# Three ring slots of 62 KiB rows in place of four of 39 KiB in a one-core decode block

## The chip, the cores and the metric

The kernel runs on one core of a Trainium2 chip, in one launch. A time is the device time of that core in microseconds (us); the time before is the median of three runs, 214.47 us (214.38 to 214.60). A profile is one execution recorded by the hardware profiler. The engines are PE (TensorE matmuls; PEld is its weight load), DVE (VectorE), ACT (ScalarE), POOL (GpSimd) and SP (SyncE), which here issues nearly all transfers. Sixteen DMA engines move the data.

## The reference

One decode step for 4 tokens: attention over the last 1024 positions of a cache with 8 key/value heads (two query heads each), then an MLP, all in float32.

```python
# x: (4, 1, 448); k_cache, v_cache: (4, 8, 4096, 256); wq: (448, 4096); wo: (4096, 448); w1: (448, 1792); w2: (1792, 448)
W = min(4096, max(256, Sk // 4))                       # 1024
q = (layernorm(x) @ wq).reshape(B, 1, 16, 256).transpose(0, 2, 1, 3)
k = repeat(k_cache[:, :, Sk - W:, :], 2, axis=1)
v = repeat(v_cache[:, :, Sk - W:, :], 2, axis=1)
p = softmax(einsum("bhqd,bhkd->bhqk", q, k) * 256 ** -0.5)
h = x + einsum("bhqk,bhkd->bhqd", p, v).transpose(0, 2, 1, 3).reshape(B, 1, 4096) @ wo
h2 = h + gelu_tanh(layernorm(h) @ w1 + b1) @ w2 + b2
```

## The kernel before

**What is loaded.** For each head g there are its keys (32 KiB per partition, `CACHE` = 8192 floats), its values (the same), a slice of wq and a slice of wo (7 KiB per partition each, `WEIGHTS` = 1792 floats). The host packs them as the kernel wants them: `kq[g - 1]` holds the keys of head g and behind them the query weights of head g + 1; `vo[g]` holds the values of head g and behind them its output weights. So a load is 128 rows of 39936 bytes, 4992 KB in all. Twelve such loads (k1, v0, k2, v1, ... k6, v5) make up the middle of the kernel.

**Where it goes.** The pool `ring` has two tags, "k" and "v", with two buffers each: four slots of 39936 bytes per partition. A load can be issued when the load that had its slot two before it has been used up. The program's order on SP is the order of the loads:

```python
    for g in range(HKV - 2):
        kt, wqt = load_k(g + 1)
        vt, wot = load_v(g)
        p, rec_next = scores(g + 1, kt)
        project_q(g + 2, wqt)
        transpose_p(g + 1, p)
        po = po_tile(g)
        values(g, vt, po)
        transposed_output(g, po, rec)
        add_output(g, wot)
        rec = rec_next
```

**What is done with it.** `scores` (line 182) multiplies the queries with the keys in two halves of 512 positions and takes the maxima (DVE); ACT makes the exponentials `p`. `project_q` (159, 165) makes the next head's queries. `transpose_p` (207) turns `p` into `pT`. `values` (219) multiplies `pT` with the values in four pairs of chunks into `po`. `transposed_output` (236, 240) scales and transposes `po` into `oT`; `add_output` (248) adds its product with the output weights to `acc`. PE runs its instructions in the order in which the program is written; the other engines' order is found by the scheduler.

**The start.** wq0 (with the transposed input), k0 (with most of the query weights of head 1) and a small rest wq1_last are loaded first.

**The end.** After the loop come k7 (4096 KB), v6 with its output weights (4992 KB), v7 in three pieces (1024, 2048, 1024 KB), its output weights wo7 (896 KB), w1 in two pieces (1792, 1344 KB) and w2 in three (1792, 896, 448 KB), all still through the four slots. PE then runs scores(7), two idle products (`keep_warm`, line 308, bf16 on zeros), the transposes of `p7`, ten idle products, values(6), the first quarter of values(7), the output of head 6, the rest of values(7), its output, the layer norm, the w1 product (388), the gelu, and the w2 product, of which chunks 0 to 7 are line 421 and chunks 8 to 13 line 431. Line 431 first needs the second piece of w2, then (from chunk 12) the third; the sum `py`, the residual `res` and the store end the kernel.

**Completion counters.** Transfers use eight completion counters in turn (DMAHW0 to DMAHW7 in the listings below); a transfer whose counter is still in use waits for the earlier transfer on it to land.

Of the kernel before, what the change touches and what calls it, by code (L numbers as in the profile page):

```python
# [8 lines left out]
F32 = mybir.dt.float32  # L9
# [3 lines left out]
AX = mybir.AxisListType  # L13
PSUM = bass.MemoryType.PSUM

B, D = 4, 448
# [3 lines left out]
F = 1792  # L20
P = 128
H = P // 2
ND = 4
# [2 lines left out]
FQ = F // 4  # L26
Q = 32
CACHE = NKC * B * DH
WEIGHTS = 4 * D
EPS = 1e-5  # L30
SCALE = DH ** -0.5

@with_exitstack
def block_kernel(ctx: ExitStack, tc, rows, wq0, k0, wq1, kq, vo, w1, w2, out):
    nc = tc.nc
    const = ctx.enter_context(tc.tile_pool(name="const", bufs=1))
    ring = ctx.enter_context(tc.tile_pool(name="ring", bufs=2))
    work = ctx.enter_context(tc.tile_pool(name="work", bufs=2))
    once = ctx.enter_context(tc.tile_pool(name="once", bufs=1))
    ps_s = ctx.enter_context(tc.tile_pool(name="ps_s", bufs=2, space=PSUM))  # L40
# [4 lines left out]

    def load(kind, src, pieces, name):
        t = ring.tile([P, CACHE + WEIGHTS], F32, tag=kind, name=name)
        at = 0  # L50
        for n in pieces:
            nc.sync.dma_start(t[:, at : at + n], src[:, at : at + n])  # L52
            at += n
        return t


    def wq_parts(t, last=None):
        parts = [(a, yT[:, a, :], slice(0, 512), t[:, a * 512 : (a + 1) * 512]) for a in range(3)]
        if last is not None:
            return parts + [(3, yT[:H, 3, :], slice(0, 512), last)]  # L60
        for i in range(2):
            parts.append((3, yT[:, 3 + i, :], slice(i * 2 * P, (i + 1) * 2 * P), t[:, 3 * 512 :]))
        return parts


    def load_k(g):
        half = CACHE // 2
        if g == 0:
            t = load("k", k0, (CACHE + 3 * 512,), "k0")


            for i in range(2):
                nc.sync.dma_start(
                    wq1_last[i * Q : (i + 1) * Q, :], wq1[i].rearrange("e (p c) -> e p c", c=512)[:, :4, :]
                )
            last = wq1_last
        else:
            pieces = (CACHE + WEIGHTS,) if g + 1 < HKV else (CACHE,)
            t = load("k", kq[g - 1], pieces, f"k{g}")
            last = None  # L80
        kt = [t[:, i * half : (i + 1) * half].rearrange("p (c b k) -> p c b k", c=2, b=B) for i in range(2)]
        return kt, wq_parts(t[:, CACHE:], last) if g + 1 < HKV else None


    def load_v(g):
        pieces = (CACHE + WEIGHTS,)
        if g == HKV - 1:
            pieces = (CACHE // 4, CACHE // 2, CACHE // 4, WEIGHTS)
        t = load("v", vo[g], pieces, f"v{g}")
        v = t[:, :CACHE].rearrange("p (c b d) -> p c b d", c=NKC, b=B)  # L90
        return [v[:, c : c + 2] for c in range(0, NKC, 2)], t[:, CACHE:].rearrange("p (j e) -> p j e", j=4)


    ident = const.tile([P, P], F32, name="ident")
# [61 lines left out]
    def project_q(g, parts):  # L156
        pq = ps_m.tile([P, 512], F32, tag="m", name=f"pq{g}")
        for j, y, cols, w in parts:
            nc.tensor.matmul(pq[j * Q : (j + 1) * Q, cols], y, w, start=True, stop=True)  # L159
# [12 lines left out]
        for i in range(2):  # L172
            nc.vector.tensor_copy(qT[g % 2][:, :, :, i * REP : (i + 1) * REP], src)

    def scores(g, kt):
        mx = work.tile([P, 2], F32, tag="mx", name=f"mx{g}")
        halves = []
        for h in range(2):
            s = ps_s.tile([P, 512], F32, tag="s", name=f"s{g}_{h}")
            for c in range(2):  # L180
                for b in range(B):
                    nc.tensor.matmul(  # L182
                        s[b * Q : (b + 1) * Q, :], qT[g % 2][:, c, b, :], kt[h][:, c, b, :],
                        start=(c == 0), stop=(c == 1),
                    )
            nc.vector.reduce_max(mx[:, h : h + 1], s, axis=AX.X)  # L186
            halves.append(s)
        nm = work.tile([P, 1], F32, tag="nm", name=f"nm{g}")
        nc.vector.tensor_max(nm, mx[:, 0:1], mx[:, 1:2])
        nc.vector.tensor_scalar_mul(nm, nm, -SCALE)  # L190
        p = work.tile([P, 2 * 512], F32, tag="p", name=f"p{g}")
        sums = work.tile([P, 2], F32, tag="sums", name=f"sums{g}")
        for h in range(2):
            nc.scalar.activation(  # L194
                p[:, h * 512 : (h + 1) * 512], halves[h], AF.Exp, bias=nm, scale=SCALE,
                accum_out=sums[:, h : h + 1],
            )
        rec = work.tile([P, 1], F32, tag="rec", name=f"rec{g}")
        nc.vector.tensor_add(rec, sums[:, 0:1], sums[:, 1:2])
        nc.vector.reciprocal(rec, rec)  # L200
        return p, rec

    def transpose_p(g, p):
        for h in range(2):
            pt = ps_t.tile([P, 4, P], F32, tag="t", name=f"ppt{g}_{h}")
            for c in range(4):
                nc.tensor.transpose(pt[:, c, :], p[:, (4 * h + c) * P : (4 * h + c + 1) * P], ident)  # L207

            src = pt.rearrange("p (c i) (b q) -> p c i b q", i=2, b=B)
            for i in range(2):  # L210
                nc.vector.tensor_copy(  # L211
                    pT[g % 2][:, 2 * h : 2 * h + 2, :, i * REP : (i + 1) * REP], src[:, :, i, :, :REP]
                )


    def values(g, vt, po, pairs=range(NKC // 2)):
        for c in pairs:
            for b in range(B):
                nc.tensor.matmul(  # L219
                    po[b * Q : (b + 1) * Q], pT[g % 2][:, c, b, :], vt[c][:, :, b, :],  # L220
                    start=(c == 0), stop=(c == NKC // 2 - 1),
                )
# [11 lines left out]
    def transposed_output(g, po, rec):  # L234
        o = work.tile([P, 2, DH], F32, tag="o", name=f"o{g}")
        nc.vector.tensor_scalar_mul(o, po, rec)  # L236
# [7 lines left out]
        nc.vector.tensor_add(dst, dst, src[:, 1, :, REP : 2 * REP])  # L244

    def add_output(g, wt):
        for i in range(4):
            nc.tensor.matmul(  # L248
                acc[i * Q : (i + 1) * Q, :], oT[g % 2][:, i, :], wt[:, i, :],
                start=(g == 0), stop=(g == HKV - 2),  # L250
            )
# [7 lines left out]
        return pool.tile([P, 2, DH], F32, tag=tag, name=f"po{g}")  # L259


    t = load("v", wq0, (WEIGHTS + ND * B,), "wq0")
    wqt = wq_parts(t[:, :WEIGHTS])
    xT = t[:, WEIGHTS : WEIGHTS + ND * B].rearrange("p (a b) -> p a b", a=ND)
# [8 lines left out]
    nc.vector.tensor_mul(yT[H:, 4, :B], d[H:, 3, :], rx[H:, :])  # L273
    project_q(0, wqt)

    kt, wqt = load_k(0)
    p, rec = scores(0, kt)
    project_q(1, wqt)
    transpose_p(0, p)
    for g in range(HKV - 2):  # L280
        kt, wqt = load_k(g + 1)
        vt, wot = load_v(g)
        p, rec_next = scores(g + 1, kt)
        project_q(g + 2, wqt)
        transpose_p(g + 1, p)
        po = po_tile(g)
        values(g, vt, po)
        transposed_output(g, po, rec)
        add_output(g, wot)
        rec = rec_next  # L290
# [12 lines left out]

# [201 lines left out]
```

## Time and profile before

| | before |
|---|---|
| median of three runs | 214.47 us |
| profiled execution, its span | 212.9 us |
| the median less the span | 1.57 us |
| scores, L182, PE busy | 42.3 us |
| values, L219, PE busy | 40.0 us |
| idle time of PE before L182 ended by a load of keys | 22.6 us |
| idle time of PE before L219 ended by a load of values | 19.6 us |
| bytes read from HBM | 88.26 MB |

The span is the time from the first to the last recorded instruction; a run's time also has what lies around it. In the timeline a row gives the start, the length, the engine, the line, the operation, the count, and in brackets the idle time of the engine just before it and what ended that. One float32 product of 128x512 shows as two matmul records, so that the 16 products of a whole `scores` or `values` are 32 records. "PEclk" in a row of stages is the clock that the throttle granted PE, 1.00 being the full one.

### The profile page before, as it was taken

How to read it: one execution, taken by the hardware profiler on the slowest of the kernel's cores; microseconds unless marked ns; L12 is line 12 of the kernel's file. 1: busy time of each engine (PE TensorE's matmuls, PEld its weight loads, DVE VectorE, ACT ScalarE, POOL GpSimd, SP SyncE). 2: the span in 40 equal slices, each digit the busy share in tenths (PEclk: the TensorE clock that was granted, in tenths of full speed). 3: DMA queues.
4: the chain of work that ended last, by engine and by line, in shares of the span. 5: the costliest groups of instructions: out<-in, count | busy, mean ns of one | idle time of the engine just before them, and what ended most of it. 6: DMA issues, size and time to landing. Idle time of an engine off the chain costs nothing.

```text
span 212.9 us, 2306 instructions
## 1 busy us (share of the span) xinstructions
PE 137.9 (65%) x971; PEld 49.1 (23%) x971; DVE 39.2 (18%) x167; ACT 21.0 (10%) x52; POOL 5.6 (3%) x17
## 2 busy tenths in 40 slices
PE   0456868093886739583986348382948476798994
PEld 0322233021231212211231113120222123234432
DVE  1420324001130202210130104110230231022320
ACT  0210213000030000300030003000030001000311
POOL 6100000000000000000000000000000000000110
PEclk9999999669597966969599859979797999699999
DMA  7999998999989999999999999999989999999991
GB/s 291 426 399 469 398 465 378 459 465 390 458 378 465 465 390 458 398 446 465 390 458 405 443 465 386 465 413 428 461 375 468 440 428 390 417 418 433 424 390 60
DMA packets 3865, 88.46 MB, mean 415 GB/s; under 512 B 448, under 2 KB 576, under 8 KB 1168
## 3 DMA queue, kind: packets, MB, share of 16 engines
q1 hardware_dynamic: 3824, 88.29, 96.9%
q8 instruction: 7, 0.11, 0.2%
q10 hardware_dynamic: 32, 0.05, 0.1%
q14 instruction: 2, 0.02, 0.0%
HBM read 88.26 MB, written 0.07 MB: 415 GB/s over the span
## 4 chain that ended last, share of the span: by engine, by line
DMA 85%; PE 11%; DVE 2%; issue 0%; SPq 0%
DMA v<-vo 65%; DMA w<-w 12%; DMA k<-k 8%; PE po L219 8%; PE acc L248 1%; DVE o L236 1%; PE pot L240 1%; PE py L431 1%; DVE oT L243 0%; DVE oT L244 0%; SPq L52 0%; DVE res L437 0%; PE py L256 0%
## 5 line engine op out<-in xcount | busy, mean ns | idle before, releaser
L182 PE MATMUL s<-k,qT 128*32 128x512 f32 x256 | 42.3, 822 | 24.7 <-DMA k<-kq 22.6
L219 PE MATMUL po<-v,pT 128*32 128x512 f32 x256 | 40.0, 772 | 19.6 <-DMA v<-vo 19.6
L186 DVE TENSOR_REDUCE mx<-s 128x1 f32<-128x512 f32 x16 | 11.1, 691 | 67.4 <-PE s L182 67.4
L182 PEld LDWEIGHTS s<-k,qT 128*32 128x32 f32 x256 | 10.0, 146 | 54.7 <-issue 29.4
L219 PEld LDWEIGHTS po<-v,pT 128*32 128x32 f32 x256 | 10.7, 135 | 42.3 <-issue 31.4
L161 ACT COPY qs<-pq 128x512 f32<-128x512 f32 x8 | 4.7, 586 | 135.8 <-PE pq L159 135.8
L236 DVE TENSOR_SCALAR o<-po,rec 128x512 f32<-128x512 f32 x8 | 6.0, 750 | 60.2 <-PE po L219 60.2
L194 ACT ACTIVATE p<-s,nm 128x512 f32<-128x512 f32 x16 | 10.9, 690 | 18.4 <-DVE nm L190 18.4
L207 PE MATMUL ppt<-ident,p 128*128 128x128 f32 x64 | 10.5, 286 | 2.0 <-ACT p L194 1.7
L165 PE MATMUL pqt<-ident,qs 128*128 128x128 f32 x32 | 5.7, 304 | 6.2 <-ACT qs L161 6.2
L240 PE MATMUL pot<-ident,o 128*128 128x128 f32 x32 | 5.2, 286 | 5.7 <-DVE o L236 5.7
L248 PE MATMUL acc<-v,oT 128*32 128x448 f32 x56 | 6.7, 551 | 3.3 <-DVE oT L244 3.3
L207 PEld LDWEIGHTS ppt<-ident,p 128*128 128x128 f32 x64 | 6.7, 140 | 6.0 <-ACT p L194 6.0
L159 PE MATMUL pq<-k,yT 128*32 128x512 f32 (+1 forms) x66 | 7.3, 515 | 0.0
L308 PE MATMUL warm<-idle 128*32 128x512 bf16 x25 | 7.3, 382 | 0.0
L240 PEld LDWEIGHTS pot<-ident,o 128*128 128x128 f32 x32 | 3.3, 140 | 13.0 <-DVE o L236 13.0
L165 PEld LDWEIGHTS pqt<-ident,qs 128*128 128x128 f32 x32 | 3.6, 150 | 10.9 <-ACT qs L161 9.1
L153 POOL TENSOR_TENSOR r<-ve_r,mhalf 128x1 f32<-128x1 f32 x2 | 1.1, 544 | 191.9 <-DVE ve_r L152 191.9
L211 DVE COPY pT<-ppt 128x16 f32<-128x16 f32 x32 | 4.7, 170 | 4.7 <-PE ppt L207 4.7
L159 PEld LDWEIGHTS pq<-k,yT 128*32 128x32 f32 x66 | 3.1, 110 | 6.1 <-issue 4.8
L138 PE MATMUL pm_x<-wq,mean 128*128 128x12 f32 x2 | 0.6, 363 | 5.8 <-DMA wq<-wq 5.8
L167 DVE TENSOR_REDUCE sm<-pqt 128x16 f32<-128x64 f32 x8 | 1.8, 225 | 13.0 <-PE pqt L165 13.0
(101 smaller groups left out, 60.9 us busy)
## 6 DMA issues: line engine op xcount, KB each, us to landing
v<-vo SPq DMA_DIRECT2D x7, 4992.0 KB, 31.8
k<-kq SPq DMA_DIRECT2D x6, 4992.0 KB, 32.0
k<-k SPq DMA_DIRECT2D x1, 4864.0 KB, 16.3
k<-kq SPq DMA_DIRECT2D x1, 4096.0 KB
w<-w SPq DMA_DIRECT2D x2, 1792.0 KB
v<-vo SPq DMA_DIRECT2D x2, 1024.0 KB, 22.2
v<-vo SPq DMA_DIRECT2D x1, 2048.0 KB
w<-w SPq DMA_DIRECT2D x1, 1344.0 KB
```

The lines of the kernel that those rows point to most:

```text
L159: nc.tensor.matmul(pq[j * Q : (j + 1) * Q, cols], y, w, start=True, stop=True)
L161: nc.scalar.copy(qs, pq)
L165: nc.tensor.transpose(pt[:, i, :], qs[:, i * P : (i + 1) * P], ident)
L182: nc.tensor.matmul(s[b * Q : (b + 1) * Q, :], qT[g % 2][:, c, b, :], kt[h][:, c, b, :], start=(c == 0), stop=(c == 1),)
L186: nc.vector.reduce_max(mx[:, h : h + 1], s, axis=AX.X)
L194: nc.scalar.activation(p[:, h * 512 : (h + 1) * 512], halves[h], AF.Exp, bias=nm, scale=SCALE, accum_out=sums[:, h : h + 1],)
L207: nc.tensor.transpose(pt[:, c, :], p[:, (4 * h + c) * P : (4 * h + c + 1) * P], ident)
L219: nc.tensor.matmul(po[b * Q : (b + 1) * Q], pT[g % 2][:, c, b, :], vt[c][:, :, b, :], start=(c == 0), stop=(c == NKC // 2 - 1),)
L236: nc.vector.tensor_scalar_mul(o, po, rec)
L240: nc.tensor.transpose(pt[:, i, c], o[:, i, c * P : (c + 1) * P], ident)
L248: nc.tensor.matmul(acc[i * Q : (i + 1) * Q, :], oT[g % 2][:, i, :], wt[:, i, :], start=(g == 0), stop=(g == HKV - 2),)
L308: nc.tensor.matmul(warm[:Q], idle[:, :Q], idle, start=True, stop=True)
```

## The change

The pool `ring` gets one tag with three buffers of 63488 bytes per partition. The keys, values and weights of three heads at a time are cut into four loads, in the order in which they are used:

| load | floats per partition | holds |
|---|---|---|
| la | 14080 (56320 bytes) | keys g+1, query weights g+2, first half of values g |
| lb | 14080 (56320 bytes) | second half of values g, output weights g, keys g+2 |
| lc | 15872 (63488 bytes) | query weights g+3, values g+1, output weights g+1, first half of keys g+3 |
| ld | 15872 (63488 bytes) | second half of keys g+3, query weights g+4, values g+2, output weights g+2 |

They run for g = 0 and g = 3: eight loads with the bytes of the twelve. The products are written in the order of the parts: `values` of a head may be split over two loads (la, lb), and `scores` likewise (lc, ld), for which `scores` is cut into `scores_half` and `softmax`. wq0 and k0 share the first slot. At the end k7 and w1 share one slot, v6 and the output weights of heads 6 and 7 a second, v7 and w2 the third. The order and the sizes of those last loads stay as they were; k7 becomes an array of its own. `p` has one buffer in place of two. The area kept for software-made DMA descriptors is set to 1024 bytes.

```diff
+HALF = CACHE // 2
 WEIGHTS = 4 * D
+SLOT = CACHE + 2 * WEIGHTS + HALF
...
-    ring = ctx.enter_context(tc.tile_pool(name="ring", bufs=2))
+    ring = ctx.enter_context(tc.tile_pool(name="ring", bufs=3))
...
-    def load(kind, src, pieces, name):
-        t = ring.tile([P, CACHE + WEIGHTS], F32, tag=kind, name=name)
+    def slot(name):
+        return ring.tile([P, SLOT], F32, tag="r", name=name)
+
+    def load(t, at, src, pieces=None):
+        dst = t[:, at : at + src.shape[-1]]
         at = 0
-        for n in pieces:
-            nc.sync.dma_start(t[:, at : at + n], src[:, at : at + n])
+        for n in pieces or (src.shape[-1],):
+            nc.sync.dma_start(dst[:, at : at + n], src[:, at : at + n])
             at += n
-        return t
+        return dst
+
+    def cut(t, sizes):
+        parts, at = [], 0
+        for n in sizes:
+            parts.append(t[:, at : at + n])
+            at += n
+        return parts
...
-        p = work.tile([P, 2 * 512], F32, tag="p", name=f"p{g}")
+        p = once.tile([P, 2 * 512], F32, tag="p", name=f"p{g}")
...
-    for g in range(HKV - 2):
-        kt, wqt = load_k(g + 1)
-        vt, wot = load_v(g)
-        p, rec_next = scores(g + 1, kt)
-        project_q(g + 2, wqt)
+    def finish(g, po, rec, wt):
+        transposed_output(g, po, rec)
+        add_output(g, output_weights(wt))
+
+    for g in (0, 3):
+        ka, kb, wqt, va = cut(load(slot(f"ta{g}"), 0, la[g // 3]), (HALF, HALF, WEIGHTS, HALF))
+        p, rec_next = scores(g + 1, [keys(ka), keys(kb)])
+        project_q(g + 2, wq_parts(wqt))
         transpose_p(g + 1, p)
         po = po_tile(g)
-        values(g, vt, po)
-        transposed_output(g, po, rec)
-        add_output(g, wot)
-        rec = rec_next
+        va = chunks(va)
+        values(g, va, po, range(0, 2))
+
+        vb, wot, ka, kb = cut(load(slot(f"tb{g}"), 0, lb[g // 3]), (HALF, WEIGHTS, HALF, HALF))
+        values(g, va + chunks(vb), po, range(2, 4))
+        p, rec_then = scores(g + 2, [keys(ka), keys(kb)])
+        finish(g, po, rec, wot)
+        transpose_p(g + 2, p)
+
+        wqt, v, wot, ka = cut(load(slot(f"tc{g}"), 0, lc[g // 3]), (WEIGHTS, CACHE, WEIGHTS, HALF))
+        project_q(g + 3, wq_parts(wqt))
+        po = po_tile(g + 1)
+        values(g + 1, chunks(v), po)
+        first_half = scores_half(g + 3, 0, keys(ka))
+        finish(g + 1, po, rec_next, wot)
+
+        kb, wqt, v, wot = cut(load(slot(f"td{g}"), 0, ld[g // 3]), (HALF, WEIGHTS, CACHE, WEIGHTS))
+        p, rec = softmax(g + 3, [first_half, scores_half(g + 3, 1, keys(kb))])
+        project_q(g + 4, wq_parts(wqt))
+        transpose_p(g + 3, p)
+        po = po_tile(g + 2)
+        values(g + 2, chunks(v), po)
+        finish(g + 2, po, rec_then, wot)
...
-    kt, _ = load_k(g + 1)
-    vt, wot = load_v(g)
-    vt_last, wo_last = load_v(g + 1)
-    t = load("k", w1, (2 * F, F + F // 2), "w1")
-    w1t = [t[:, a * F : min((a + 1) * F, 3 * F + F // 2)] for a in range(ND)]
-    t = load("k", w2, (8 * D, 4 * D, 2 * D), "w2")
-    w2t = [t[:, c * D : (c + 1) * D] for c in range(NFC)]
+    e = [slot(f"te{i}") for i in range(3)]
+    kt = [keys(t) for t in cut(load(e[0], 0, k7), (HALF, HALF))]
+    v, wot = cut(load(e[1], 0, vo[0]), (CACHE, WEIGHTS))
+    vt, wot = chunks(v), output_weights(wot)
+    vt_last = chunks(load(e[2], 0, vo[1][:, :CACHE], (CACHE // 4, CACHE // 2, CACHE // 4)))
+    wo_last = output_weights(load(e[1], CACHE + WEIGHTS, vo[1][:, CACHE:]))
+    w1t = cut(load(e[0], CACHE, w1, (2 * F, F + F // 2)), (F, F, F, F // 2))
+    w2t = cut(load(e[2], CACHE, w2, (8 * D, 4 * D, 2 * D)), NFC * (D,))
```

Two places of the order matter below. The first is SP's queue from the last loads of the loop to the last piece of v7. A row gives the line, the operation, the tile and its source, and what the issue waits for: DMAHW is a completion counter, PE that engine's progress. Before:

```order
L52 DMA k6_719<-kq 128x9984 [waits DMAHW6_49,PE_49]
L52 DMA v5_721<-vo 128x9984 [waits DMAHW7_49,PE_49]
L52 DMA k7_815<-kq 128x8192 [waits DMAHW0_49,PE_49]
L52 DMA v6_817<-vo 128x9984 [waits DMAHW1_49,PE_49]
L52 DMA v7_819<-vo 128x2048 [waits DMAHW3_49,PE_49]
```

And with the change:

```order
L57 DMA tc3_669<-lc 128x15872 [waits DMAHW6_49,DMAHW3_49,PE_49]
L57 DMA td3_729<-ld 128x15872 [waits DMAHW7_49,DMAHW4_49,PE_49]
L57 DMA te0_813<-k7 128x8192 [waits DMAHW5_49,PE_49]
L57 DMA te1_814<-vo 128x9984 [waits DMAHW6_49,PE_49]
L57 DMA te2_815<-vo 128x2048 [waits DMAHW7_49,PE_49]
```

The first piece of v7 (te2) takes over the slot of td3, the last load of the loop, and is issued when PE has done the last product that reads td3; before it took the slot of v5.

The second place is PE's queue from the last load of the loop to scores(7). Before, with k6 the load of keys 6 and v5 that of values 5:

```order
L182 MATMUL s6_0_724<-k6_719,qT0_111 32x512 x8
L182 MATMUL s6_1_734<-k6_719,qT0_111 32x512 x8
L159 MATMUL pq7_754<-k6_719,yT_97 32x512 x3
L159 MATMUL pq7_754<-k6_719,yT_97 32x256 x2
L165 MATMUL pqt7_762<-ident_84,qs7_760 128x128 x4
L207 MATMUL ppt6_0_771<-ident_84,p6_747 128x128 x4
L207 MATMUL ppt6_1_778<-ident_84,p6_747 128x128 x4
L219 MATMUL po5_785<-v5_721,pT1_114 32x512 x16
L240 MATMUL pot5_804<-ident_84,o5_802 128x128 x4
L248 MATMUL acc_133<-v5_721,oT1_116 32x448 x4
L182 MATMUL s7_0_832<-k7_815,qT1_112 32x512 x8
```

And with the change, from the first product that reads td3:

```order
L174 MATMUL s6_1_731<-td3_729,qT0_111 32x512 x8
L154 MATMUL pq7_752<-td3_729,yT_97 32x512 x3
L154 MATMUL pq7_752<-td3_729,yT_97 32x256 x2
L160 MATMUL pqt7_760<-ident_84,qs7_758 128x128 x4
L206 MATMUL ppt6_0_769<-ident_84,p6_745 128x128 x4
L206 MATMUL ppt6_1_776<-ident_84,p6_745 128x128 x4
L218 MATMUL po5_783<-td3_729,pT1_114 32x512 x16
L239 MATMUL pot5_802<-ident_84,o5_800 128x128 x4
L247 MATMUL acc_133<-td3_729,oT1_116 32x448 x4
L174 MATMUL s7_0_827<-te0_813,qT1_112 32x512 x8
```

The sequence is the same but for the first half of scores(6), which now comes from tc3. What moved is what it waits for: before, the first seven rows followed k6 and the next three v5; now everything from the second half of scores(6) to the last product of head 5 follows td3, whose bytes are those of the end of k6 and all of v5.

More of the change, by code (lines that the diff above doesn't have):

```diff
@@ L33, in block_kernel @@
 @with_exitstack
-def block_kernel(ctx: ExitStack, tc, rows, wq0, k0, wq1, kq, vo, w1, w2, out):
+def block_kernel(ctx: ExitStack, tc, rows, wq0, k0, wq1, la, lb, lc, ld, k7, vo, w1, w2, out):
     nc = tc.nc
     const = ctx.enter_context(tc.tile_pool(name="const", bufs=1))
-    ring = ctx.enter_context(tc.tile_pool(name="ring", bufs=2))
+    ring = ctx.enter_context(tc.tile_pool(name="ring", bufs=3))
     work = ctx.enter_context(tc.tile_pool(name="work", bufs=2))
@@ L63, in wq_parts, with keys, chunks, output_weights @@
         return parts
[L66 to L91, printed above, removed]
+    def keys(t):
+        return t.rearrange("p (c b k) -> p c b k", c=2, b=B)
+    def chunks(t):
+        v = t.rearrange("p (c b d) -> p c b d", b=B, d=DH)
+        return [v[:, c : c + 2] for c in range(0, v.shape[1], 2)]
+    def output_weights(t):
+        return t.rearrange("p (j e) -> p j e", j=4)
     ident = const.tile([P, P], F32, name="ident")
@@ L173, in project_q, with scores_half, softmax @@
             nc.vector.tensor_copy(qT[g % 2][:, :, :, i * REP : (i + 1) * REP], src)
[L175 to L187, printed above, removed]
+    def scores_half(g, h, kt):
+        s = ps_s.tile([P, 512], F32, tag="s", name=f"s{g}_{h}")
+        for c in range(2):
+            for b in range(B):
+                nc.tensor.matmul(
+                    s[b * Q : (b + 1) * Q, :], qT[g % 2][:, c, b, :], kt[:, c, b, :],
+                    start=(c == 0), stop=(c == 1),
+                )
+        m = work.tile([P, 1], F32, tag=f"mx{h}", name=f"mx{g}_{h}")
+        nc.vector.reduce_max(m, s, axis=AX.X)
+        return s, m
+    def softmax(g, parts):
+        halves, mx = zip(*parts)
         nm = work.tile([P, 1], F32, tag="nm", name=f"nm{g}")
-        nc.vector.tensor_max(nm, mx[:, 0:1], mx[:, 1:2])
+        nc.vector.tensor_max(nm, mx[0], mx[1])
         nc.vector.tensor_scalar_mul(nm, nm, -SCALE)
-        p = work.tile([P, 2 * 512], F32, tag="p", name=f"p{g}")
+        p = once.tile([P, 2 * 512], F32, tag="p", name=f"p{g}")
         sums = work.tile([P, 2], F32, tag="sums", name=f"sums{g}")
@@ L197, in scores @@
             )
-        rec = work.tile([P, 1], F32, tag="rec", name=f"rec{g}")
+        rec = work.tile([P, 1], F32, tag=f"rec{g % 3}", name=f"rec{g}")
         nc.vector.tensor_add(rec, sums[:, 0:1], sums[:, 1:2])
@@ L201, in scores @@
         return p, rec
+    def scores(g, kt):
+        return softmax(g, [scores_half(g, h, kt[h]) for h in range(2)])
     def transpose_p(g, p):
@@ L259, in po_tile @@
         return pool.tile([P, 2, DH], F32, tag=tag, name=f"po{g}")
-    t = load("v", wq0, (WEIGHTS + ND * B,), "wq0")
-    wqt = wq_parts(t[:, :WEIGHTS])
-    xT = t[:, WEIGHTS : WEIGHTS + ND * B].rearrange("p (a b) -> p a b", a=ND)
+    t = slot("t0")
+    wqt, xT = cut(load(t, 0, wq0), (WEIGHTS, ND * B))
+    wqt = wq_parts(wqt)
+    xT = xT.rearrange("p (a b) -> p a b", a=ND)
+    ka, kb, wqt1 = cut(load(t, WEIGHTS + ND * B, k0), (HALF, HALF, 3 * 512))
+    for i in range(2):
+        nc.sync.dma_start(
+            wq1_last[i * Q : (i + 1) * Q, :], wq1[i].rearrange("e (p c) -> e p c", c=512)[:, :4, :]
+        )
     d = work.tile([P, ND, B], F32, tag="d", name="d_x")
@@ L274, in block_kernel @@
     project_q(0, wqt)
-    kt, wqt = load_k(0)
-    p, rec = scores(0, kt)
-    project_q(1, wqt)
+    p, rec = scores(0, [keys(ka), keys(kb)])
+    project_q(1, wq_parts(wqt1, wq1_last))
     transpose_p(0, p)
-    for g in range(HKV - 2):
-        kt, wqt = load_k(g + 1)
-        vt, wot = load_v(g)
-        p, rec_next = scores(g + 1, kt)
-        project_q(g + 2, wqt)
+    def finish(g, po, rec, wt):
[5 more added lines that the diff above has]
+        project_q(g + 2, wq_parts(wqt))
@@ L467 @@
     wo = np.asarray(A_wo).reshape(HKV, 4, P, D).transpose(0, 2, 1, 3).reshape(HKV, P, 4 * D)
-    kq = np.concatenate([k[1:], np.concatenate([wq[2:], wq[:1]])], axis=2)
+    ka, kb = k[..., :HALF], k[..., HALF:]
+    va, vb = v[..., :HALF], v[..., HALF:]
+    la = np.concatenate([k[1:5:3], wq[2:6:3], va[0:4:3]], axis=2)
+    lb = np.concatenate([vb[0:4:3], wo[0:4:3], k[2:6:3]], axis=2)
+    lc = np.concatenate([wq[3:7:3], v[1:5:3], wo[1:5:3], ka[3:7:3]], axis=2)
+    ld = np.concatenate([kb[3:7:3], wq[4:8:3], v[2:6:3], wo[2:6:3]], axis=2)
     k0 = np.concatenate([k[0], wq[1][:, : 3 * 512]], axis=1)
@@ L472 @@
     wq1 = np.concatenate([wq1, np.zeros((2, 8, 512), np.float32)], axis=2)
-    vo = np.concatenate([v, wo], axis=2)
+    vo = np.concatenate([v[6:], wo[6:]], axis=2)
     w1 = packed(np.asarray(B_w1))
@@ L489 @@
     arrays = {
-        "rows": rows, "wq0": np.concatenate([wq[0], xT], axis=1), "k0": k0, "wq1": wq1, "kq": kq, "vo": vo, "w1": w1, "w2": w2,
+        "rows": rows, "wq0": np.concatenate([wq[0], xT], axis=1), "k0": k0, "wq1": wq1, "la": la, "lb": lb, "lc": lc, "ld": ld, "k7": k[7], "vo": vo, "w1": w1, "w2": w2,
     }
     arrays = {n: np.ascontiguousarray(a) for n, a in arrays.items()}
-    nc = bacc.Bacc("TRN2", target_bir_lowering=False, num_devices=1)
+    nc = bacc.Bacc("TRN2", target_bir_lowering=False, num_devices=1, dynamic_dma_scratch_size=1024)
     args = [
```

## The prediction

> **What bounds the kernel now.** I read the page first: busy time, the slices, the queues and the chain.
>
> ```profile
> span 212.9 us, 2306 instructions
> PE 137.9 (65%) x971; PEld 49.1 (23%) x971; DVE 39.2 (18%) x167; ACT 21.0 (10%) x52; POOL 5.6 (3%) x17
> DMA  7999998999989999999999999999989999999991
> q1 hardware_dynamic: 3824, 88.29, 96.9%
> q8 instruction: 7, 0.11, 0.2%
> DMA 85%; PE 11%; DVE 2%; issue 0%; SPq 0%
> ```
>
> The DMA engines are busy from the second slice to the last but one, and SP's queue alone fills 96.9% of them; PE is busy for 65%. Where the chain names PE in the loop, the DMA line shows no hole beside it: PE's progress lets a later load be issued, while others are being carried. So the transfers set the time, as long as a load is always waiting behind the one under way. The stages show the same, two of the middle for all (us, then PE, PEld, DVE, ACT, POOL, granted clock, DMA share, GB/s):
>
> ```profile
> 54.00:66.00 12.00, 9.18 (x54) 3.10 (x54) 2.87 (x13) 1.94 (x5) 0.00 (x0) 0.77 1.00 431
> 101.00:113.00 12.00, 9.34 (x54) 3.10 (x54) 2.87 (x13) 1.94 (x5) 0.00 (x0) 0.74 1.03 443
> ```
>
> Then the end, from the chain in order of time, the timeline, and the waits for the tile py:
>
> ```profile
> 182.14 26.22 DMA w<-w
> 208.37 0.04 issue
> 208.41 0.35 PEld L431 LDWEIGHTS py<-w,gT 128*32 128x32 f32 x16 [1.20 <-DMA w<-w]
>   DMA w<-w: 1.6, 2
> ```
>
> Line 431 waits twice for w2: 1.20 us for its second piece, and 1.6 - 1.2 = 0.4 us for its third. So the last transfers end the kernel, but PE is only some 0.4 us ahead of them. Two clocks have to be kept apart: when the last bytes land, and when PE's own sequence, which starts with values(6) on the landing of v6, is through.
>
> **Part 1, the loads.** The bytes stay: 12 x 4992 = 59904 KB before, and 4 x 7040 + 4 x 7936 = 59904 KB (rows of 56320 and 63488 bytes) now. What goes is what a load costs beside its bytes, four times. Landings are read from PE's first product on each load (k6, v5, k7, v6):
>
> ```profile
> 148.81 5.06 PE L182 MATMUL s<-k,qT 128*32 128x512 f32 x32 [3.53 <-DMA k<-kq]
> 160.63 5.34 PE L219 MATMUL po<-v,pT 128*32 128x512 f32 x32 [3.11 <-DMA v<-vo]
> 170.33 3.64 PE L182 MATMUL s<-k,qT 128*32 128x512 f32 x32 [1.40 <-DMA k<-kq]
> 182.26 6.20 PE L219 MATMUL po<-v,pT 128*32 128x512 f32 x40 [2.62 <-DMA v<-vo]
> k<-kq SPq DMA_DIRECT2D x6, 4992.0 KB, 32.0
> k<-kq SPq DMA_DIRECT2D x1, 4096.0 KB
> ```
>
> A load of 4992 KB takes 160.63 - 148.81 = 11.82 us and one of 4096 KB 170.33 - 160.63 = 9.70 us: 2.12 us for 896 KB, or 2.366 us per 1000 KB, which leaves 11.82 - 11.81 = 0.01 us that doesn't go with the bytes. The chain's last piece gives a second equation: 26.22 us for the eight loads between the landing of v6 and that of w2's second piece, 10816 KB. With 11.82 = 4992 x + f and 26.22 = 10816 x + 8 f, f is 0.105 us. So four loads fewer save 0.04 to 0.42 us. I take the middle, 0.06 us each, **0.24 us**. That rows of 63488 bytes move at the rate of those of 39936 isn't shown; rows of 32768 and 39936 move alike, and I take the same rate (the other end is a rival).
>
> [...]
>
> **Part 2, the ring.** With three slots a load is issued when the one three places before it is used up, with two loads queued or under way. At 2.366 us per 1000 KB the new loads take 16.66 and 18.78 us, so a slot has some 35 us from its landing until the queue is dry. The work on one load is 13.6 us (td3, worked out below; the others have the same products within one half of scores or values). That leaves over 20 us, and I cost the loss of the fourth slot at nothing in the loop. The tight place is the end, where the load behind td3 that needs its slot, v7's first piece, has only k7 and v6 ahead: 9088 KB, 21.5 us.
>
> **Part 3, PE after td3.** Before, PE did scores(6) to the transposes of p6 on k6, and only values(5) and the output of head 5 on v5. Now all of it but half of scores(6) comes behind td3, whose last byte is that of v5: 160.63 - 0.24 = 160.39. The rows for its length, and for what follows:
>
> ```profile
> 153.69 1.04 PE L159 MATMUL pq<-k,yT 128*32 128x512 f32 x10
> 156.19 1.32 PE L207 MATMUL ppt<-ident,p 128*128 128x128 f32 x8
> 167.97 0.96 PE L248 MATMUL acc<-v,oT 128*32 128x448 f32 x8 [0.47 <-DVE oT L244]
> 168.99 1.75 SPq L52 DMA_DIRECT2D v<-vo  x4
> 173.79 0.59 PE L308 MATMUL warm<-idle 128*32 128x512 bf16 x2
> 177.31 2.33 PE L308 MATMUL warm<-idle 128*32 128x512 bf16 x10
> 187.66 0.75 DVE L236 TENSOR_SCALAR o<-po,rec 128x512 f32<-128x512 f32 x1 [9.98 <-PE po L219]
> 160.63:165.97 5.34, 5.34 (x32) 1.26 (x32) 0.00 (x0) 0.00 (x0) 0.00 (x0) 0.68 1.00 430
> 170.33:173.79 3.46, 3.46 (x33) 1.03 (x33) 0.69 (x1) 0.00 (x0) 0.00 (x0) 1.00 0.91 392
> 173.79:182.23 8.44, 4.17 (x24) 1.82 (x19) 1.70 (x9) 1.45 (x4) 0.00 (x0) 1.00 0.96 411
> 182.23:187.60 5.37, 5.34 (x36) 1.90 (x40) 0.00 (x0) 0.00 (x0) 0.00 (x0) 0.68 1.00 426
> ```
>
> A full scores or values of 32 records takes 3.46 us at a granted clock of 1.00, and 5.34 us at 0.68, as it does behind an idle time of 2.6 us and more. Behind td3:
>
> - half of scores(6), PE coming from an idle time: 1.7 us at the full clock, 3.4 at half of it. I take 3.4: 163.8.
> - project_q(7), the softmax and the transposes of p6: from 153.69 to 156.19 + 1.32 = 157.51, 3.82 us: 167.6.
> - values(5), now at the full clock, since PE has been at work for 7 us: 3.46: 171.1.
> - the output of head 5: from 165.97 to 167.97 + 0.96 = 168.93, 2.96 us: 174.0. That is 13.6 us after the landing.
>
> So v7's first piece is issued at 174.1, not at 168.99. It must arrive before v6 has been carried, at 182.26 - 0.24 = 182.02. From issue to first bytes it is at most 2.8 us (wq0's 904 KB landed 4.9 us after issue, of which 2.1 are its bytes):
>
> ```profile
> wq<-wq SPq DMA_DIRECT2D x1, 904.0 KB, 4.9
> ```
>
> That leaves about 5 us, and the wait costs nothing. The pieces of w1 and w2 stand behind it on SP; they go out by 178 or, by their counters, when v6 and v7's first piece land, with transfers until 200 ahead of them.
>
> Then PE: scores(7) finds k7 landed (170.1) and runs 174.0 to 177.5 instead of 170.33 to 173.79. To the end of the ten idle products it is 177.31 + 2.33 - 173.79 = 5.85 us more: 183.35. So **values(6) starts 1.1 us later** than the 182.26 of before. But it came behind 2.62 us of idle time then and ran 5.34 us at a clock of 0.68; now the longest idle time ahead of it is the 1.67 us of the softmax, after which the stage 173.79:182.23 kept a clock of 1.00. At 3.46 us it ends at 186.8, and the scaling of o starts at 186.9, 0.76 us before the 187.66 of now. From there PE, DVE and ACT do what they did, with the loads of v7, w1 and w2 landing 0.24 us earlier. It may start as late as 187.66 - 0.24 + 0.4 = 187.8 before the transfers cease to set the end. So part 3 costs nothing, covered by 0.9 us; with the cover gone each us later is a us at the end.
>
> The split of values and scores adds no instruction on PE; the maxima go to two tiles, the same count on DVE. The single buffer of p delays nothing: the transposes of one head are done a load before the exponentials of the next.
>
> **Sum.** -0.24 + 0 + 0 = -0.24 us: the span goes from 212.9 to 212.7. The median lies 1.57 us above the span, which stays: 214.47 - 0.24 = **214.2 us**.
>
> **Rivals.**
>
> *PE comes late at the end (slower).* If the throttle reads the 1.67 us of softmax(7) as idle, or td3's half of scores(6) warms the clock too late, values(6) runs at 0.68 again: 5.34 - 3.46 = 1.9 us more, o at 188.8, 1.0 us past the 187.8, and the time is 214.2 + 1.0 = 215.2. For it: PE is 1.1 us late at that point, and the cover is only 0.9. Against it: the same softmax gap kept the clock at 1.00. [...] 17%.
>
> *A load's fixed cost is larger (faster).* The best rate of a stage above is 443 GB/s; at it 4992 KB (5.11 MB) would take 11.54 us, 0.28 us less than a load does. If that were all fixed cost, four loads would save 1.1 us: 213.3. Against it is the 9.70 us of the smaller load. [...]
>
> *Long rows are slower.* 1% off the rate of the 59904 KB (141.7 us) costs 1.4 us: 215.6. Against it is that 32768 and 39936 bytes go alike; for it, that nothing in the trace is longer. 9%.
>
> *The queue runs dry before v7.* It needs td3's work 5 us longer than worked out, 18.6 us, or starvation in the loop. At 2 us of hole: 216.2. 5%.
>
> **How the numbers follow.** The forecast has 57%, with a range of its own of 213.8 to 214.6: the fixed cost from both sides, and the seven instruction fetches (16 KB each, 0.6 us at 26 GB/s on one DMA engine), which may fall on an engine that is ahead or on the one that ends last. Less than 0.2% (0.43 us) can't be told from no change by a measurement of this kernel. Of the 57, 13 lie beyond that on the fast side, 3 on the slow one. Faster: 13 + 12 = 25%. Slower: 3 + 14 of the 17 + 9 + 5 = 31%. Within 0.2%: 44%. The range from 213.7 to 215.3 leaves out half of the larger fixed cost, most of the slow rows and the dry queue, and the worst of PE's lateness.
>
> **What would show it.** Right: DMA at 9 in all slices of the middle with SP's queue near 96.9%; eight loads landing 16.6 to 16.7 and 18.7 to 18.8 us apart; td3 landing near 160.4; v7's issue near 174; values(6) starting near 183.3 and running some 3.5 us at a clock of 1.00; line 459 (431 before) still waiting for w2, at 208.2. Wrong: no wait for w2 there and o after 187.8 (PE late); loads further apart (long rows slower) or closer (larger fixed cost); a slice of DMA below 9 near 180 (dry queue).

## The result and the profile after

The change takes 215.2 us (median of 22 runs, 214.62 to 216.22) where the kernel before takes 214.56: the ratio is 1.0032, 95% interval 1.0022 to 1.0042. It is slower by 0.64 us by the medians, 0.69 by the ratio, where 0.24 us less was forecast. The runs of the change are spread over 1.6 us, ten from 214.62 to 215.0 and twelve from 215.15 to 216.22; those of the kernel before keep within 0.4 us but for two.

The profiled execution is one of the shorter ones (214.81 us). The page, in the lines that answer to those shown of before:

```profile
span 213.0 us, 2294 instructions
PE 137.4 (64%) x971; PEld 48.2 (23%) x971; DVE 38.4 (18%) x167; ACT 21.2 (10%) x52; POOL 5.6 (3%) x17
DMA  7999899999999999999999999999999998999990
q1 hardware_dynamic: 3248, 88.29, 96.7%
DMA 64%; PE 29%; DVE 3%; ACT 1%; issue 1%; SPq 0%; ACTq 0%; DVEq 0%
```

One slice of the middle, 176 to 181 us, reads 8, near the place where the prediction looked for a dry queue. It is no hole that counts: nothing behind it landed late, as seen below, and the kernel before has three such slices. The bytes are the same, and there are 576 packets fewer. What is new is the chain: PE's share rose from 11% to 29%, at the cost of DMA's. The rows from the landing of td3 on, in the timeline:

```profile
160.19 3.64 PE L174 MATMUL s<-td,qT 128*32 128x512 f32 x16 [5.78 <-DMA td<-ld]
163.60 1.93 PE L154 MATMUL pq<-td,yT 128*32 128x512 f32 x10
173.84 0.96 PE L247 MATMUL acc<-td,oT 128*32 128x448 f32 x8 [0.47 <-DVE oT L243]
174.62 3.62 PE L174 MATMUL s<-te,qT 128*32 128x512 f32 x32
181.57 2.33 PE L336 MATMUL warm<-idle 128*32 128x512 bf16 x10
183.97 4.50 PE L218 MATMUL po<-te,pT 128*32 128x512 f32 x40
187.67 0.75 DVE L235 TENSOR_SCALAR o<-po,rec 128x512 f32<-128x512 f32 x1 [5.74 <-PE po L218]
207.83 0.35 PEld L459 LDWEIGHTS py<-te,gT 128*32 128x32 f32 x16 [0.65 <-DMA te<-w]
207.83 0.64 PE L459 MATMUL py<-te,gT 128*32 128x128 f32 x16
208.12 0.53 ACT L453 COPY pas<-pa 128x448 f32<-128x448 f32 x1 [1.56 <-PE pa L449]
208.70 0.43 PE L255 MATMUL py<-pas,sel 128*32 128x128 f32 x8 [0.23 <-ACT pas L453]
```

td3 landed at 160.19, 0.44 us before v5 did. But values(6) starts at 183.97, 1.7 us after the 182.26 of before, and has no wait for v6 in front of it. The products of line 459 (431 before) have no wait for w2 in front of them either. Their weight load (PEld) still waits for it for 0.65 us, but PE is at the products of line 449 until then and loses next to nothing: it starts line 459 1.54 us after line 449, and 1.50 us after it in a run below where nothing waited for w2. The wait that counts is the one of line 255, for ACT's copy of the sum that PE made on line 449. So PE's own sequence, not the transfers, now ends the kernel. And one row of SP's waits at the very end, of before and then of after:

```profile
SPq L499 <- DMA out<-res: 0.9, 1, 0.9
```

```profile
SPq L532 <- DMA out<-res: 1.2, 1, 1.2
```

The residual is added 0.14 us earlier than before (210.07 against 210.21), yet the span is 0.1 us longer: what follows the store takes 0.25 us more.

### The profile page after: what moved, and what is told of

Its sections match the earlier page's. It is cut to its first block, busy times and chain, and to the rows that moved or that the text cites. A ratio compares the mean times of both kernels' runs of the same rounds, so it can differ in the third digit from the quotient of the medians.

```text
span 213.0 us, 2294 instructions
## 1 busy us (share of the span) xinstructions
PE 137.4 (64%) x971; PEld 48.2 (23%) x971; DVE 38.4 (18%) x167; ACT 21.2 (10%) x52; POOL 5.6 (3%) x17
## 4 chain that ended last, share of the span: by engine, by line
DMA 64%; PE 29%; DVE 3%; ACT 1%; issue 1%; SPq 0%; ACTq 0%; DVEq 0%
DMA ta<-la 21%; DMA td<-ld 20%; DMA tb<-lb 16%; PE s L174 8%; DMA t<-k 8%; PE po L218 8%; PE ppt L206 2%; PE pu L416 2%; PE warm L336 1%; PE acc L247 1%; PE pq L154 1%; PE pot L239 1%; PE pa L449 1%; DVE o L235 1%; DVE mx L179 1%
## 5 line engine op out<-in xcount | busy, mean ns | idle before, releaser
L174 PE MATMUL s<-ta,qT 128*32 128x512 f32 x64 | 12.2, 935 | 8.9 <-DMA ta<-la 8.9
L174 PE MATMUL s<-td,qT 128*32 128x512 f32 x32 | 7.3, 1061 | 12.0 <-DMA td<-ld 12.0
L218 PE MATMUL po<-tb,pT 128*32 128x512 f32 x32 | 7.3, 1061 | 10.4 <-DMA tb<-lb 10.4
L154 PE MATMUL pq<-tc,yT 128*32 128x512 f32 (+1 forms) x20 | 3.9, 890 | 14.8 <-DMA tc<-lc 14.8
L218 PE MATMUL po<-tc,pT 128*32 128x512 f32 x64 | 10.5, 815 | 0.0
L174 PE MATMUL s<-tb,qT 128*32 128x512 f32 x64 | 9.1, 717 | 0.0
L218 PE MATMUL po<-te,pT 128*32 128x512 f32 x64 | 7.9, 596 | 0.1
L174 PE MATMUL s<-t,qT 128*32 128x512 f32 x32 | 6.1, 925 | 2.6 <-DMA t<-k 2.6
L218 PE MATMUL po<-td,pT 128*32 128x512 f32 x64 | 7.3, 595 | 0.0
L174 PEld LDWEIGHTS s<-ta,qT 128*32 128x32 f32 x64 | 2.9, 163 | 17.4 <-issue 14.4
```

Of the source, the lines that this page charges most:

```text
L174: nc.tensor.matmul(s[b * Q : (b + 1) * Q, :], qT[g % 2][:, c, b, :], kt[:, c, b, :], start=(c == 0), stop=(c == 1),)
L218: nc.tensor.matmul(po[b * Q : (b + 1) * Q], pT[g % 2][:, c, b, :], vt[c][:, :, b, :], start=(c == 0), stop=(c == NKC // 2 - 1),)
```

## The experiments

The times of before beside them are 214.50, 214.53 and 214.54 us (29 to 33 runs each). In parentheses stand the ratio to the kernel before and its 95% interval, then the range of the runs. All edits but those named b are to the change. An idle product (`keep_warm`) multiplies zeros and only keeps PE at work.

**Is it PE?** Ten idle products more ahead of values(6), 2.3 us of PE's time, first in the change, then in the kernel before:

```diff
-    keep_warm(10, warm0)
+    keep_warm(20, warm0)
```

> The change with twenty idle products ahead of values(6) where it has ten: 2.3 us more of PE. Theory A: PE sets the end, so the time rises by 2.3 us to 217.5. Theory B: PE has room, no change, 215.2 us.

Measured: 217.43 us (214.5 before it; ratio 1.014, 1.0123 to 1.0157), 2.2 us more than the change. In its profile values(6) starts 2.15 us later (186.12) and the span is 215.2 us for 213.0.

> The kernel before with twenty idle products ahead of values(6) where it has ten: the same 2.3 us that e4_twenty adds to the change. Theory A: before the change PE waits 2.6 us for v6 at that point, so the products fill that wait and the transfers still set the end: no change, 214.4 to 214.6 us (e4_twenty: 2.3 us more than the change). If PE's work counted as much in the kernel before: 216.8 us.

Measured: 214.76 us (1.0010, 1.0001 to 1.0019), 0.2 us more, somewhat over what was expected, a tenth of the products' time. So the same work costs its full length in the change and nearly nothing in the kernel before. PE sets the end of the change; theory B, that PE has room there, falls.

**Which part of PE's time?** Twenty idle products in the 5.8 us that PE idles ahead of td3:

```diff
         finish(g + 1, po, rec_next, wot)
+        if g == 3:
+            keep_warm(20, ps_t.tile([P, 512], F32, tag="t", name="warm_c"))
```

> The change with twenty idle products on PE between the work on tc3 and the landing of td3, a stretch in which PE idles (154.4 to 160.2 us in the trace of the change). Theory A (PE comes late at the end because the work behind td3 starts at half the clock): half of scores(6) and project_q(7) run at the full clock, PE is 2 us or more earlier at values(6), the transfers set the end again, 214.2 to 214.5 us, and the runs lie within 0.4 us of each other. Theory B (the transfers with longer rows set the end): no change, 215.2 us with the same spread.

Measured: 214.82 us (1.0017, 1.0007 to 1.0026), from 214.51 to 215.85. Half the loss is gone, the spread is not: the expectation was missed. The timeline of one of its shorter runs (214.54 us) shows why:

```profile
160.15 1.92 PE L174 MATMUL s<-td,qT 128*32 128x512 f32 x16 [1.57 <-DMA td<-ld]
161.89 1.05 PE L154 MATMUL pq<-td,yT 128*32 128x512 f32 x10
177.71 1.32 PE L206 MATMUL ppt<-ident,p 128*128 128x128 f32 x8 [1.68 <-ACT p L190]
178.97 4.02 PE L291 MATMUL warm<-idle 128*32 128x512 bf16 x10
183.05 4.50 PE L218 MATMUL po<-te,pT 128*32 128x512 f32 x40
207.91 0.64 PE L461 MATMUL py<-te,gT 128*32 128x128 f32 x16 [0.38 <-DMA te<-w]
```

td3's first products now run at the full clock (1.00 from 160 to 166 us; 1.92 and 1.05 us for 3.64 and 1.93), but the ten idle products take 4.02 us for 2.33: behind the 1.68 us in which PE waits for the exponentials of head 7 the clock was halved (a mean of 0.72 from 178 to 184 us, 1.00 in the stages on either side). In this run the transfers still set the end, and show where it lies: 207.91, 0.50 us before the 208.41 of the kernel before.

Without the ten idle products:

```diff
-    keep_warm(10, warm0)
```

> The change without the ten idle products ahead of values(6), which take PE 2.33 us. Theory A: PE reaches values(6) 2.3 us earlier, about when v6 lands, 214.2 to 214.6 us. Theory B: 215.2 us.

Measured: 214.89 us (1.0019, 1.0006 to 1.0033), 214.36 to 215.74. The median misses what was expected. The lower runs are there, and again the spread: in its profile, a run of 215.36 us, values(6) with the first quarter of values(7) takes 7.18 us for 4.50. Without the ten products PE comes there earlier, but with its clock still halved behind the gap in the softmax (0.50 from 180.47 to 187.30).

**The gap in the softmax.** Nine idle products for two between scores(7) and the transposes of p7:

```diff
-    keep_warm(2, warm0)
+    keep_warm(9, warm0)
```

> The change with nine idle products in place of two in the softmax of head 7, which fill the 1.68 us in which PE waits for the exponentials. Theory A1 (two things make PE late: the half clock behind td3 in every run, and in some runs a drop of the clock that this gap brings, as in e1_warm, where the ten idle products behind it took 4.02 us and not 2.33): the slow runs go, the fast ones stay, 214.6 to 214.9 us within 0.4 us. If the gap has no part in it: 215.2 us and the spread of the change (214.6 to 216.2).

Measured: 214.71 us (1.0008, 0.9999 to 1.0017), 214.54 to 215.15: the upper runs are gone but for two, at 215.11 and 215.15, a spread of 0.6 us where 0.4 was expected. With the twenty products as well:

> e1_warm and e9_gap together: PE at work from tc3 to values(6) without a gap over 1 us. Theory A1: the clock stays full, values(6) starts on the landing of v6, the transfers set the end in all runs: 214.2 to 214.3 us, within 0.3 us of each other. Theory B (longer rows or other transfers set the end): as e1_warm, 214.8 us.

Measured: 214.49 us (1.0003, 0.9994 to 1.0011), 214.36 to 215.05, some 0.2 us over what was expected and more than twice as wide. Its profiled run was one of its longer ones (214.95). There the twenty products had ended 2.27 us ahead of td3, and td3's first products ran slow again (2.73 and 1.95 us), but that isn't why it is long: PE waits for w2 at the end (0.39 us, until 208.00). Some 0.3 us are the store itself, for which SP waits longer than the 1.2 us of the change:

```profile
SPq L534 <- DMA out<-res: 1.5, 1, 1.5
```

Why this store took longer is open.

**What do the longer runs of the change look like?** The change itself, run three times more:

> The change itself, another look. Theory A1: the span goes with the start of values(6) and its length: near 212.9 where the ten idle products take 2.33 us and values(6) with the first quarter of values(7) 4.5 us, above 213.4 where one of them runs at half the clock (4.0 us, or 6 us and more). If the transfers vary: the landing of td3 is later by as much as the span is longer.

> The change itself, another look, for a run that may fall otherwise; each theory expects the same as for a1_again.

> The change itself, a third look, for a run that may fall otherwise; each theory expects the same as for a1_again.

Measured: 215.70, 215.75 and 214.81 us, spans of 213.9, 214.0 and 213.0. td3 landed at 160.28, 160.16 and 160.24, so the transfers are the same. The third is like the profile above. The first, in the timeline and in two stages of 3.41 us (PE's busy time first, the granted clock before the DMA share):

```profile
163.69 1.07 PE L155 MATMUL pq<-td,yT 128*32 128x512 f32 x10
180.80 4.01 PE L337 MATMUL warm<-idle 128*32 128x512 bf16 x10
184.86 4.50 PE L219 MATMUL po<-te,pT 128*32 128x512 f32 x40
208.68 0.64 PE L460 MATMUL py<-te,gT 128*32 128x128 f32 x16
209.59 0.43 PE L256 MATMUL py<-pas,sel 128*32 128x128 f32 x8 [0.27 <-ACT pas L454]
```

```profile
177.36:180.77 3.41, 1.72 (x14) 0.85 (x9) 1.45 (x7) 1.45 (x4) 0.00 (x0) 1.00 0.83 353
180.77:184.18 3.41, 3.41 (x9) 1.18 (x9) 0.26 (x2) 0.00 (x0) 0.00 (x0) 0.51 1.03 435
```

The ten idle products take 4.01 us: PE was at work for only 1.72 of the 3.41 us before them, and its clock was halved for the next 3.41. The shorter run, of the profile after, has the same gap of 1.68 us. Its clock changes at 165.96 us. In this profile and in that of before, the changes of the clock (16 from 32.84 to 165.96 us, and 22 from 39.08 to 185.85 us) lie whole multiples of 3.41 us apart. Counted on from 165.96 in such steps, the gap (178.64 to 180.32) falls into two stretches:

```profile
162.55:165.96 3.41, 2.98 (x18) 0.75 (x10) 1.01 (x3) 0.34 (x1) 0.00 (x0) 0.50 1.01 428
176.20:179.61 3.41, 2.44 (x22) 0.58 (x14) 1.70 (x4) 0.12 (x1) 0.00 (x0) 1.00 1.00 431
179.61:183.03 3.42, 2.70 (x15) 1.53 (x16) 0.69 (x6) 1.33 (x4) 0.00 (x0) 1.00 0.92 385
```

PE is at work for 2.44 and 2.70 us of them, and the clock stays at 1.00. Five profiles (the first and second of these runs, e1_warm, e2_noten, and b3_split of below) have the whole gap inside one stretch, with 1.72 or 1.73 us of work, and in all five the next stretch shows a clock of 0.50 or 0.51. So where the gap fell decided in these profiles.

In the first run values(6) starts at 184.86, 0.9 us after that of the shorter run, and line 256 runs at 209.59, 0.9 us after 208.70: the whole difference of the spans. The second has the same rows (4.02 us, 184.91). In these runs project_q(7) ran at or near the full clock (1.07 and 1.22 us for 1.93), so they were 0.8 us ahead until the softmax, and lost 1.7 there. The runs above 215.9 were not caught in a profile; what they lose besides is open.

**One lump or two.** The last long load brought in two, the keys and query weights ahead of the values:

```diff
-        kb, wqt, v, wot = cut(load(slot(f"td{g}"), 0, ld[g // 3]), (HALF, WEIGHTS, CACHE, WEIGHTS))
+        kb, wqt, v, wot = cut(load(slot(f"td{g}"), 0, ld[g // 3], (HALF + WEIGHTS, CACHE + WEIGHTS) if g else None), (HALF, WEIGHTS, CACHE, WEIGHTS))
```

> The change with td3 brought in two loads (half of the keys of head 6 and the query weights of head 7, then the values and output weights of head 5): scores(6), project_q(7) and the transposes of p6 can be done some 9 us before the values land, as before the change. Theory A: PE is through with head 5 about 4 us earlier and waits for k7 again, the transfers set the end, 214.3 to 214.6 us (one load more than the change, the store's counter one place later). Theory B: 215.2 us or a little more.

Measured: 214.46 us (0.9998, 0.9989 to 1.0007), 214.35 to 214.63. Nothing is added on PE, and both the loss and the spread are gone. So the lump is what makes PE late, and where the clock falls sets by how much: with the lump left whole and PE kept at work, e7_both came to 214.49 us. The timeline of e5_parts:

```profile
160.49 3.64 PE L218 MATMUL po<-td,pT 128*32 128x512 f32 x32 [0.54 <-DMA td<-ld]
170.06 5.16 PE L174 MATMUL s<-te,qT 128*32 128x512 f32 x32 [2.98 <-DMA te<-k]
182.00 4.50 PE L218 MATMUL po<-te,pT 128*32 128x512 f32 x40 [1.09 <-DMA te<-vo]
207.96 0.64 PE L459 MATMUL py<-te,gT 128*32 128x128 f32 x16 [0.37 <-DMA te<-w]
```

PE waits for k7, for v6 and for w2 again.

**The store's counter.** Four loads of 4 bytes at the start move the store to another of the eight completion counters: from the fourth to the last in the change, from the last to the fourth in the kernel before.

```diff
+    tiny = const.tile([1, 4], F32, name="tiny")
+    for j in range(4):
+        nc.scalar.dma_start(tiny[:, j : j + 1], rows[j, :1, :1])
```

> The change with four loads of 4 bytes at the start on ACT's queue, so that the store of the result has the last of the eight completion counters again, as before the change. Theory C (behind the store SP looks at the counters one by one; with the store on the fourth of them four looks of 0.06 us follow its landing instead of preceding it): 0.25 us less than the change, 214.95 us, and the spread of the change stays. If the counter doesn't matter: 215.2 us.

Measured: 215.09 us (1.0028, 1.0014 to 1.0043), 214.22 to 215.88. Within the spread of the change this can't be told from it. (Its profile caught a short run, 214.22 us.)

> The kernel before with four loads of 4 bytes at the start on ACT's queue, which move the store of the result from the last completion counter to the fourth, where the change has it. Theory C: four looks of 0.06 us follow the landing of the store, 0.25 us more, 214.75 us. If the counter doesn't matter: 214.5 us.

Measured: 214.87 us (1.0014, 1.0005 to 1.0022), 214.71 to 214.99: 0.33 us more (0.11 to 0.47), four loads of 4 bytes included, and SP's last wait is that of the change:

```profile
SPq L502 <- DMA out<-res: 1.2, 1, 1.2
```

**What a load costs.** Eight of the loads of the kernel before cut in two:

```diff
-        pieces = (CACHE + WEIGHTS,)
+        pieces = (CACHE + WEIGHTS,) if g > 3 else (CACHE // 2, CACHE // 2 + WEIGHTS)
```

(and the same for k1 to k4)

> The kernel before with eight of its twelve loads (k1 to k4, v0 to v3) cut in two, on the same rows: eight loads more, no byte more, the store's counter unchanged. It prices a load: at the 0.06 us of the prediction 0.5 us more (215.0), at the 0.11 us by which td3 landed earlier than v5 per load saved 0.9 us more (215.4); at nothing, 214.5 us.

Measured: 215.15 us (1.0027, 1.0018 to 1.0036): 0.61 us for eight, **0.076 us each**. Its first product on k6 stands at 149.42, 0.61 us behind the 148.81 of before, so all of it is in the transfers.

**Versions that beat both.** e7_both with the little loads, and e5_parts with three of them:

> e7_both with e3_counter: PE without gaps and the store on the last completion counter. Theories A1 and C: 0.25 us below e7_both, 214.0 us, faster than the kernel before by 0.5 us, which is what the four loads fewer bring when nothing takes it away. If the counter does nothing: as e7_both.

Measured: 214.31 us (0.9989, 0.9981 to 0.9998), 214.14 to 214.59: 0.18 us below e7_both, where 0.25 was expected, and so not down to 214.0.

> e5_parts with three loads of 4 bytes at the start, so that the store has the last counter: the change with its last long load brought in two and nothing added on PE. Theories A and C: 0.2 us below e5_parts (214.46), so 214.26 us, 0.25 us below the kernel before, with as narrow a spread.

Measured: 214.23 us (0.9987, 0.9978 to 0.9996), 214.16 to 214.65, 0.3 us below the kernel before. In its profile the end waits for w2 (207.93), and SP for the store for 0.9 us:

```profile
207.93 0.64 PE L462 MATMUL py<-te,gT 128*32 128x128 f32 x16 [0.39 <-DMA te<-w]
```

```profile
SPq L535 <- DMA out<-res: 0.9, 1, 0.9
```

## Why the prediction was wrong

**Part 1 was right in kind and too small in size.** The transfers gained 0.44 us at td3 and 0.50 us at w2, where 0.24 was taken from a range of 0.04 to 0.42. The measured cost of a load accounts for 4 x 0.076 = 0.30 us of it. The rest is for the most part the profile of before, one of its longer runs: its span is 212.9 us, and the median of 32 runs beside b1_twenty is 212.7. b1_twenty and b2_counter, with the same long loads, have w2 at 208.18 and 208.19, and to these the gain is 0.28 us. Rows of 63488 bytes are not slower: tc3 and td3 landed 18.75 us apart (141.44 and 160.19), where 18.78 was foreseen at the old rate. That rival falls, and so does that of a larger fixed cost, the 12 in the sum of the chances for faster: it needed 0.28 us for a load, which no run shows, and b3_split shows 0.076.

**Part 2 held.** The loads kept their pace through the loop, and v7's wait for td3 cost nothing: PE was done with td3 at 174.8, against 174.0 foreseen, and w2 landed as early as in e5_parts, where td3's work ended sooner (line 459 at 207.83 and 207.96).

**Part 3 failed**, in the sentence "So part 3 costs nothing, covered by 0.9 us". The 0.9 us lay between the scaling of o, foreseen at 186.9, and the latest harmless start, 187.8. Both ends were wrong.

PE came later than foreseen. The half clock behind td3 (0.50 from 155.72 to 165.96 us) lasted, in the profile, through project_q(7) too (1.93 us for 1.04), values(6) began at 183.97 for 183.35, and o at 187.67, 0.77 us late. That is still ahead of 187.8, so the sign named for a late PE did not show in this run; PE ended the kernel all the same. (In a1_again, a longer run of the change, o started at 188.57.)

The latest harmless start came earlier than foreseen. The prediction read PE's lead over the transfers from line 431's last wait for w2, some 0.4 us. But line 256 also needs ACT's copy of PE's sum, and in the kernel before that copy was hardly ahead:

```profile
208.15 0.53 ACT L425 COPY pas<-pa 128x448 f32<-128x448 f32 x1 [1.62 <-PE pa L421]
208.78 0.48 PE L256 MATMUL py<-pas,sel 128*32 128x128 f32 x8
```

It ended at 208.68 and was used at 208.78, so the lead was 0.1 us at most. And between these profiles the transfers gained 0.50 us, not 0.24. In e1_warm, where the transfers set the end, line 255 runs at 208.28; in the change it runs 21.03 us after o (187.67 and 208.70). So o had to start by 208.28 - 21.03 = 187.25, and at 187.67 it was 0.4 us late.

In the longer runs the gap in the softmax comes on top. The stage 173.79:182.23 of the kernel before was read as showing that 1.67 us of waiting leaves the clock alone. It showed one run; in the five profiles with the gap inside one 3.41 us stretch, PE worked for 1.72 or 1.73 us of it and the clock was 0.50 or 0.51 in the next.

With values(6) at 183.97 the residual was added 0.14 us before the 210.21 of before; the transfers would have allowed 0.50. With values(6) at 184.86 it was added at 210.96. So PE takes back between 0.36 us and some 1.3 us of what the loads save.

**The sum left out a term.** What follows the store inside the span was taken as fixed, without a word. Four transfers fewer moved the store from the last completion counter to the fourth, 0.25 us more in the profile; b2_counter prices that move at 0.33 us (0.11 to 0.47).

From profile to profile, for the shorter runs then: -0.50 + 0.36 + 0.25 = 0.1 us more, the span of 213.0 for 212.9; for the longer ones 0.9 us on top, 213.9. Against the usual span of before, 212.7, both differences are 0.2 us larger. The rival "PE comes late at the end" had both causes, the slow start behind td3 and the gap in the softmax. It had the loss in values(6), which ran its 4.50 us at the full clock in the profiles of the change; the loss fell on project_q(7) and on the ten idle products. That its 215.2 us is the measured median is luck: it left out the store and ACT's copy, put 0.24 us for the landings, and the profiled runs took 214.81, 215.70 and 215.75 us. It was given 17% because the half clock behind td3 was taken to end with its first products, and the gap was judged by a single run.

## What to carry to other kernels

Where the transfers and the engine behind them end within half a microsecond of each other, as here, fewer and larger loads trade 0.08 us each (b3_split) for work that can't start until a larger lump has landed: keep the last loads small, since there the lump's work can no longer be caught up (cutting only the last one in two took the change from 215.2 to 214.46 us). Measure a cover against every wait at the end, not only the longest: here ACT's copy was 0.1 us ahead where w2 seemed to leave 0.4. A cover that is smaller than one halved stretch costs (1.7 us here) was not safe against a wait of 1.68 us, behind which the clock was halved in five profiles. And count what follows the last store when the number of transfers changes (0.25 us more here).

## What the runs showed of the hardware

Two things were not expected. PE's clock was halved for 3.41 us (for 6.83 in e2_noten) after a stretch of 3.41 us in which PE was at work for 1.72 or 1.73 us, in five profiles of five with the gap of the softmax inside one stretch; filling the 1.68 us gap with seven more idle products narrowed the runs from between 214.62 and 216.22 us to between 214.54 and 215.15. How much work keeps the clock isn't shown: in the profile before it stayed at 1.00 behind a stretch with 1.74 us of work (110.76 to 114.17), and b2_counter has one with 1.46 us (178.16 to 181.57), all of it idle products, behind which it stayed at 1.00 too. And what follows the store went with the completion counter that the store has: in the profiles with the store on the fourth counter SP's wait shows 1.2 us, with the store on the last 0.9 us, but for two in which the store itself took some 0.3 us longer (e7_both and e8_all). SP's looks at the counters, grouped by their line, with the first and last start behind the durations, before and after:

```profile
L499 SPq EVENT_SEMAPHORE  x7: 17/28/28, 210.9 to 212.9; - x7
```

```profile
L532 SPq EVENT_SEMAPHORE  x7: 17/28/28, 212.0 to 213.0; - x7
```

Before, the first of them passed at 210.9 us, while the store was under way; in the change the first was done only at 212.0 us, behind the store, and the others followed it, four of them some 0.06 us apart. From the start of the residual to the end of the span it is 2.7 us before and 2.96 us in the change.
